# Fillers that spread the moving tiles of a fused attention and MLP kernel over eight byte remainders modulo 256

## The chip, the cores and the metric

The kernel runs on one core of a Trainium2 chip. The metric is the device time of one execution in microseconds: the median of three runs, 985.93 us, with 985.16 and 987.45 as the lowest and the highest. One more execution was profiled; every duration below comes from that one.

## The reference

Block-causal attention (4 batches, 8 heads, 576 tokens, head size 64), then a gated MLP with a sigmoid (512 to 1536 to 512), then an MLP with a leaky ReLU (512 to 2048 to 512), all in float32:

```python
scores = scale * np.matmul(q, k.transpose(0, 1, 3, 2))
scores = np.where(block_i >= block_j, scores, -1000000000.0)   # blocks of 64 positions
attn = np.exp(scores - np.max(scores, axis=-1, keepdims=True))
attn = attn / (np.sum(attn, axis=-1, keepdims=True) + 1e-09)
x = np.matmul(attn, v)            # then laid out as 2304 tokens x 512
x = (1.0 / (1.0 + np.exp(-(x @ w_gate))) * (x @ w_val)) @ w_out
h = x @ w_in
out = np.maximum(0.01 * h, h) @ w_out2
```

## The kernel before

The 2304 tokens lie along the columns of every tile, the features along the 128 partitions. They are worked on in three stages, of 768, 512 and 1024 tokens (the third as two halves of 512 that are combined by Strassen's scheme). The attention of a later batch is woven into the matmuls of the stage before it.

Every float32 number of the MLPs is split into a high and a low part of type `float32r`, side by side in one tile, and each product is three matmuls: high by high, high by low, low by high. The function `half_unit` issues twelve of them for one output tile of stages one and two (four slices of the inner dimension, line 1301); `pair_unit` issues six for one Strassen product of the third stage (line 1149). In each of these matmuls a 128x128 piece of the weight tile `w` is the stationary operand, loaded anew for every matmul, and 512 columns (256, 320 or 192 at some places of stage one) of another tile are the moving operand. Attention (`attention`, lines 428, 569, 584, 633, 657, 730, 753, 773) uses plain float32; in its transposes `ident` is moving and `both` is stationary.

A planner (`Plan.order`) sets the order of all instructions from costs and due times in the code. It knows nothing of addresses.

The tiles are allocated one pool after the other, each starting where the last one ended, in multiples of 32 bytes of a partition. `pool` and `ring` make the pools; `const` is the pool of the constants (`ident`, `mask`, `x1`, `warm`). Two fillers are there already: `warm`, of which one column is used, has 64 columns, and a pool `even` of 192 bytes stands ahead of `r_x`. With them every weight tile and every moving tile of the MLPs starts at a multiple of 256 bytes of its partition. All slices that the MLP matmuls read start at multiples of 256 bytes within their tile, and so do the slices of `w`.

Of the kernel before, what the change touches and what calls it, by code (L numbers as in the profile page):

```python
# [8 lines left out]
F32 = mybir.dt.float32  # L9
# [9 lines left out]
P = 128  # L19
# [205 lines left out]
def block_attention_then_two_mlps(  # L225
# [30 lines left out]
    def pool(name, bufs, **k):  # L256
        return ctx.enter_context(tc.tile_pool(name=name, bufs=bufs, **k))

    def ring(name, bufs, shape, dtype=F32, **k):
        return Ring(pool("p_" + name, bufs, **k), bufs, shape, dtype, name)  # L260

    out_hbm = out
    const = pool("const", 1)
    dram = pool("dram", 1, space=bass.MemoryType.DRAM)
    r_raw = ring("raw", 3, [P, 8 * P], U32)
    r_mag = ring("mag", 2, [P, 4 * P])
    r_rnd = ring("rnd", 2, [P, 4 * P], I32)
    r_wf = ring("wf", 3, [P, 4 * P])
    r_w = ring("w", 7, [P, 2, 4 * P], F32R)
    r_g = ring("g", 4, [P, 2 * SL], F32R)  # L270
    r_gf = ring("gf", 3, [P, SL])
    r_qk = ring("qk", 3, [P, 2, S])
    r_v = ring("v", 2, [P, 2, NKT, D])
# [9 lines left out]

    ident = const.tile([P, P], F32, name="ident")
    mask = const.tile([P, 4 * P + BLK], BF16, name="mask")
    x1 = const.tile([P, 4, 2, TN], F32R, name="x1")
    warm = const.tile([P, 64], F32, name="warm")
    pool("even", 1).tile([P, 48], F32, name="even")
    r_x = ring("x0", 4, [P, 2 * TN])
    r_xa = ring("xa", 2, [P, 4 * CUT])  # L290
    x0, xa, xt = [r_x.tile(F32R) for _ in range(4)], [r_xa.tile(F32R) for _ in range(2)], []
    r_sg = ring("sg", 1, [P, NSG[0] * SL])
    sg = [r_sg.tile()]

    N_PT = (NKT - 1) * 2 * 4 * P
    r_both = ring("both", 1, [P, 16 * TN])
    both = r_both.tile()
    p_t = Lazy(lambda: both[:, :N_PT].rearrange("p (j a q) -> p j a q", j=NKT - 1, a=2))

    pp, at_col = {}, N_PT  # L300
    for c, n, turns_of in ((0, P, 2), (1, 2 * P, 2), (2, 3 * P, 1), (3, 4 * P, 1), (NKT - 1, S, 1)):
# [4 lines left out]
    assert at_col <= 16 * TN  # L306
    for k, x in (("first", (3, 0, 0)), ("second", (3, 1, 0))):
        pp[k] = pp[x]
    r_acc = ring("acc", 1, [P, 4 * SL])
    acc = r_acc.tile()  # L310
    wd = [dram.tile([P, 2, 4 * P], F32, name=f"wd{u}") for u in range(NU)]
# [1193 lines left out]
```

## Time and profile before

| | us |
|---|---|
| median of three runs | 985.93 |
| the profiled execution, its own time | 985.49 |
| its span, first to last instruction | 983.7 |
| TensorE matmul busy (PE) | 968.5 |
| TensorE weight load busy (PEld) | 780.4 |
| VectorE busy (DVE) | 777.4 |
| ScalarE busy (ACT) | 549.6 |
| GpSimd busy (POOL) | 163.1 |
| granted TensorE clock, mean | 1.000 |

Consecutive matmuls overlap in the pipeline, so the duration of one (389 ns for 512 columns) is longer than the distance from its start to the next one's start. The distance is what a matmul costs; it is read from the start times in the timeline, where equal instructions that follow each other are merged into one row with their count.

### The profile page before, as it was taken

Reading aid. Unit: us, or ns where it says so; the run is one execution under the profiler, and the core shown is the slowest. Engines: PE = TensorE matmul, PEld = TensorE weight load, DVE = VectorE, ACT = ScalarE, POOL = GpSimd, SP = SyncE. Lnnn points to the kernel's source line nnn. Section 1 sums busy time; section 2 is a strip of 40 time slices with the busy share of each in tenths; the row PEclk is TensorE's granted clock in tenths of the full one; section 3 lists DMA queues with packets and bytes.
Section 4 is the critical chain, followed back from the end, with each engine's and each line's share of the span. In section 5 each row is a group of like instructions: output and inputs, shape, how many; then the busy total and the mean of one; then the engine's idle time right before and its main releaser. Section 6 shows DMA issues by size and latency. Waiting matters only on the chain.

```text
span 983.7 us, 15675 instructions
## 1 busy us (share of the span) xinstructions
PE 968.5 (98%) x5468; PEld 780.4 (79%) x5468; DVE 777.4 (79%) x1658; ACT 549.6 (56%) x1103; POOL 163.1 (17%) x172
## 2 busy tenths in 40 slices
PE   7999999999999999999999999999999999999998
PEld 4688888879888888778777877778888877888886
DVE  6989989889989847778789988985538479958656
ACT  7988776576766516455655575444526134744521
POOL 2422001221102101213432232120002021100000
PEclk9999999999999999999999999999999999999999
DMA  7488886856875636989888887877565555665664
GB/s 212 139 288 268 265 288 218 265 186 227 277 266 188 214 121 232 311 278 296 302 283 282 290 262 252 294 255 249 179 204 194 189 183 160 200 212 182 198 195 147
DMA packets 92718, 227.52 MB, mean 231 GB/s; under 512 B 9952, under 2 KB 29920, under 8 KB 92640
## 3 DMA queue, kind: packets, MB, share of 16 engines
q1 hardware_dynamic: 92640, 226.53, 69.6%
q8 instruction: 43, 0.70, 0.3%
q14 instruction: 35, 0.29, 0.1%
HBM read 150.47 MB, written 76.02 MB: 230 GB/s over the span
## 4 chain that ended last, share of the span: by engine, by line
PE 94%; DVE 2%; ACT 2%; DMA 1%; issue 0%; SPq 0%; ACTq 0%; DVEq 0%
PE mm L1301 47%; PE sc L1149 18%; PE tp L1149 9%; PE mm L1149 4%; PE tp L633 3%; PE sc L428 3%; PE pa L657 2%; PE tp L428 2%; PE tp L569 1%; DMA w<-ds 1%; PE mm L657 1%; PE tp L584 1%; ACT both L500 1%; ACT both L518 1%; DVE x L1221 0%; DMA qk<-in_qk 0%
## 5 line engine op out<-in xcount | busy, mean ns | idle before, releaser
L1301 PE MATMUL mm<-x,w 128*128 128x512 f32 (+2 forms) x1008 | 234.2, 384 | 0.0
L1301 PEld LDWEIGHTS mm<-x,w 128*128 128x128 f32 x1008 | 179.9, 188 | 38.5 <-issue 5.2
L1301 PE MATMUL mm<-g,w 128*128 128x512 f32 (+1 forms) x792 | 163.7, 358 | 0.0
L1301 PEld LDWEIGHTS mm<-g,w 128*128 128x128 f32 x792 | 130.2, 189 | 23.0 <-issue 2.4
L1149 PE MATMUL sc<-both,w 128*128 128x512 f32 x480 | 128.2, 390 | 0.1
L1149 PEld LDWEIGHTS sc<-both,w 128*128 128x128 f32 x480 | 89.9, 188 | 19.9 <-ACT wf L342 0.5
L500 ACT ACTIVATE both<-both,nm 128x256 f32<-128x256 f32 (+5 forms) x148 | 84.1, 570 | 28.3 <-DVE nm L485 27.6
L901 POOL TENSOR_TENSOR wf<-mag,rnd 128x512 int32<-128x512 int32 x28 | 37.3, 1332 | 205.9 <-DVE w L355 107.2
L887 ACT ACTIVATE mag<-raw 128x512 f32<-128x512 f32 x68 | 45.6, 671 | 42.8 <-POOL wf L901 18.1
L1301 PE MATMUL mm<-xa,w 128*128 128x256 f32 x480 | 63.6, 285 | 0.0
L1301 PEld LDWEIGHTS mm<-xa,w 128*128 128x128 f32 x480 | 60.8, 191 | 3.3 <-issue 0.8
L355 DVE TENSOR_TENSOR g<-gf,g 128x512 fp32r<-128x512 f32 (+2 forms) x73 | 56.8, 779 | 3.0 <-ACT g L342 3.0
L520 POOL TENSOR_SCALAR both<-both,r 128x256 f32<-128x256 f32 (+6 forms) x54 | 34.9, 653 | 114.3 <-DVE r L513 95.7
L342 ACT ACTIVATE g<-gf 128x512 fp32r<-128x512 f32 (+2 forms) x61 | 40.0, 657 | 24.1 <-DVE gf L1332 12.7
L518 ACT ACTIVATE both<-both,r 128x384 f32<-128x384 f32 (+6 forms) x94 | 48.7, 567 | 7.1 <-DVE r L513 7.0
L485 DVE CUSTOM_DVE_ANT_0 both<-sc,mask 128x256 f32<-128x256 f32 (+6 forms) x101 | 39.4, 423 | 16.1 <-PE sc L428 16.1
L1362 DVE TENSOR_TENSOR acc<-mm,acc 128x512 f32<-128x512 f32 (+1 forms) x60 | 35.8, 598 | 18.8 <-PE mm L1301 18.6
L1221 DVE TENSOR_TENSOR x<-sc,x 128x512 f32<-128x512 f32 x44 | 30.1, 689 | 22.3 <-PE sc L1149 22.2
L895 DVE SCALAR_TENSOR_TENSOR mag<-raw,mag 128x512 int32<-128x512 int32 x68 | 47.4, 698 | 0.3
L1301 PE MATMUL mm<-sg,w 128*128 128x512 f32 (+1 forms) x216 | 47.2, 354 | 0.0
L428 PE MATMUL sc<-qk 64*128 64x384 f32 (+5 forms) x228 | 41.9, 415 | 5.1 <-DMA qk<-in_qk 5.1
L355 DVE TENSOR_TENSOR w<-wf,w 128x512 fp32r<-128x512 f32 x68 | 46.5, 684 | 0.2
(255 smaller groups left out, 1843.7 us busy)
## 6 DMA issues: line engine op xcount, KB each, us to landing
w<-wd SPq DMA_DIRECT2D x102, 512.0 KB, 4.6
raw<-in_w SPq DMA_DIRECT2D x68, 512.0 KB, 4.4
wd<-w SPq DMA_DIRECT2D x68, 512.0 KB, 4.1
ds<-raw SPq DMA_DIRECT2D x68, 512.0 KB, 5.2
w<-ds SPq DMA_DIRECT2D x68, 512.0 KB, 4.3
qk<-in_qk SPq DMA_DIRECT2D x32, 288.0 KB, 5.7
w<-wd SPq DMA_DIRECT2D x68, 128.0 KB, 3.8
v<-in_v SPq DMA_DIRECT2D x32, 160.0 KB, 3.5
```

Source lines behind the costliest of these rows:

```text
L342: nc.scalar.activation(dst(), src(), AF.Copy)
L355: engines[e].tensor_tensor(dst(), a(), f32(b()), ALU.subtract)
L428: nc.tensor.matmul(ps[row:row + nq, col:col + nk], lhsT=tqk[half, 0, q0:q0 + nq], rhs=tqk[half, 1, k0:k0 + nk], start=True, stop=True,)
L485: nc.vector.tensor_tensor_reduce(out=pt[:, n:n + width], in0=ps[:, col:col + width], in1=mask[:, 4 * P + BLK - width:] if masked else mask ...
L500: nc.scalar.activation(pt[:, :n], pt[:, :n], AF.Exp, bias=nm[:, k - 1:k], scale=-1.0, accum_out=sm[:, i:i + 1],)
L518: nc.scalar.activation(pt[:, :n], pt[:, :n], AF.Copy, scale=r[:, i:i + 1])
L887: op("act", c_act(n), lambda: nc.scalar.activation(mag[:], words(1).bitcast(F32), AF.Abs), [raw], [mag], [raw, mag], d - 8)
L895: op("dve", c_dve(n), lambda: nc.vector.scalar_tensor_tensor(out=mag[:].bitcast(I32), in0=words(1).bitcast(I32), scalar=-0x40000000, in1=m ...
L901: engines[e].tensor_tensor(wf[:].bitcast(I32), mag[:].bitcast(I32), rnd[:], ALU.add)
L1149: nc.tensor.matmul(p[:, :n], lhsT=wt[:, wl, at * P:(at + 1) * P], rhs=view[:, xl], start=first and k == 0 and wl + xl == 0, stop=k == 1 an ...
L1301: nc.tensor.matmul(ps[:, :n], lhsT=ws[:, wl, k * P:(k + 1) * P], rhs=srcs[k]()[:, xl, hs], start=k == 0 and wl + xl == 0, stop=k == 3 and ...
L1362: op("dve", c_dve(n), lambda: nc.vector.tensor_tensor(a(), ps[:, :n], a(), ALU.add), [ps], toks_a, [ps, *host], e)
```

## The change

No instruction is added, removed or moved, and no tile changes its place in the order of allocation except `x1` and `warm`, which swap. A helper `gap(n)` opens a pool with one tile of n bytes per partition that nothing uses. `warm` shrinks to 32 columns. The fillers shift the tiles as in this table (byte addresses follow from the sizes of the tiles in order; "moving" counts the matmuls of the two MLPs that read the tile as moving operand):

| tile | start modulo 256 before | after | moving, 512 columns | moving, fewer columns |
|---|---|---|---|---|
| `w` (stationary) | 0 | 0 | - | - |
| `x1` | 0 | 128 | 720 | - |
| `g` | 0 | 192 | 762 | 264 of 256 |
| `x0` | 0 | 160 | 432 | 48 of 320, 48 of 192 |
| `xa` | 0 | 32 | 120 | 480 of 256 |
| `sg` | 0 | 64 | 186 | 72 of 256 |
| `both` | 0 | 96 | 480 | - |
| `acc` | 0 | 224 | 102 | - |
| `qk`, `raw` | 0 | 0 | 210 | - |

`x0` and `x1` both appear as `x` in the rows of the profile. In attention the moving tiles `qk`, `last` and `ident` and the stationary tile `v` keep their remainders (0, 128, 128, 0); `both` goes to 96 there too.

```diff
+    def gap(n):
+        pool(f"gap{len(gaps)}", 1).tile([P, n // 4], F32, name=f"gap{len(gaps)}")
+        gaps.append(n)
+
+    gaps = []
...
     r_w = ring("w", 7, [P, 2, 4 * P], F32R)
+    gap(192)
     r_g = ring("g", 4, [P, 2 * SL], F32R)
+    gap(64)
     r_gf = ring("gf", 3, [P, SL])
...
     mask = const.tile([P, 4 * P + BLK], BF16, name="mask")
+    warm = const.tile([P, 32], F32, name="warm")
     x1 = const.tile([P, 4, 2, TN], F32R, name="x1")
-    warm = const.tile([P, 64], F32, name="warm")
-    pool("even", 1).tile([P, 48], F32, name="even")
+    const.tile([P, 32], F32, name="gap")
+    gap(352)
     r_x = ring("x0", 4, [P, 2 * TN])
+    gap(128)
     r_xa = ring("xa", 2, [P, 4 * CUT])
...
+    gap(32)
     r_sg = ring("sg", 1, [P, NSG[0] * SL])
...
+    gap(32)
     r_both = ring("both", 1, [P, 16 * TN])
...
+    gap(128)
     r_acc = ring("acc", 1, [P, 4 * SL])
```

## Rows read from the trace of the kernel before

**Rows 1.** The page: span, busy time of the engines, granted clock in 40 slices.
```profile
span 983.7 us, 15675 instructions
PE 968.5 (98%) x5468; PEld 780.4 (79%) x5468; DVE 777.4 (79%) x1658; ACT 549.6 (56%) x1103; POOL 163.1 (17%) x172
...
PEclk9999999999999999999999999999999999999999
```

**Rows 2.** The chain that ended last, and the longest waits of PE: total us, times, longest.
```profile
PE 94%; DVE 2%; ACT 2%; DMA 1%; issue 0%; SPq 0%; ACTq 0%; DVEq 0%
...
PE sc L428 <- DMA qk<-in_qk: 5.1, 2, 4.8
PE tp L1149 <- DMA w<-ds: 2.1, 2, 1.6
PE tp L1149 <- DVE x L355: 0.9, 1, 0.9
```

**Rows 3.** Groups of matmuls by shape: xcount | busy us, mean ns of one.
```profile
L1301 PE MATMUL mm<-x,w 128*128 128x512 f32 x912 | 220.8, 394 | 0.0
...
L1149 PE MATMUL sc<-both,w 128*128 128x512 f32 x480 | 128.2, 390 | 0.1
L1301 PE MATMUL mm<-xa,w 128*128 128x256 f32 x480 | 63.6, 285 | 0.0
```

**Rows 4.** Timeline of PE, third stage: start us, us, instruction, xcount.
```profile
838.00 0.84 PE L1149 MATMUL mm<-x,w 128*128 128x512 f32 x3
838.68 2.88 PE L1149 MATMUL sc<-both,w 128*128 128x512 f32 x12
841.40 0.84 PE L1149 MATMUL tp<-xa,w 128*128 128x512 f32 x3
842.08 0.84 PE L1149 MATMUL mm<-x,w 128*128 128x512 f32 x3
...
852.28 0.84 PE L1149 MATMUL sc<-g,w 128*128 128x512 f32 x3
852.96 0.84 PE L1149 MATMUL tp<-qk,w 128*128 128x512 f32 x3
853.64 0.84 PE L1149 MATMUL sc<-both,w 128*128 128x512 f32 x3
...
859.76 0.84 PE L1149 MATMUL tp<-raw,w 128*128 128x512 f32 x3
860.44 0.84 PE L1149 MATMUL sc<-both,w 128*128 128x512 f32 x3
```

**Rows 5.** Timeline of PE, first stage, units of 256 and 512 columns in turn.
```profile
162.99 2.91 PE L1301 MATMUL mm<-x,w 128*128 128x512 f32 x12
165.74 1.59 PE L1301 MATMUL mm<-xa,w 128*128 128x256 f32 x12
167.17 2.91 PE L1301 MATMUL mm<-x,w 128*128 128x512 f32 x12
```

**Rows 6.** Duration ns min/median/max of one matmul, line 1301, from 100 to 143 us.
```profile
L1301 PE MATMUL mm<-x,w x72: 389/389/398, 100.0 to 123.5; 128*128 128x512 f32 x72
L1301 PE MATMUL mm<-xa,w x68: 277/283/386, 99.8 to 142.9; 128*128 128x256 f32 x68
```

**Rows 7.** Weight loads of the third stage, 835 to 975 us, by shape.
```profile
L1149 PEld LDWEIGHTS sc<-both,w 128*128 128x128 f32 x174 | 32.7, 188 | 6.8
```

**Rows 8.** Timeline of PE: attention scores of 288 columns, first at 0, then at 128.
```profile
32.26 0.70 PE L428 MATMUL sc<-qk 64*64 64x288 f32 x4
32.80 0.65 PE L428 MATMUL pa<-qk 64*64 64x288 f32 x4
```

**Rows 9.** Timeline, end of the program: last sum and the stores of the output.
```profile
978.32 2.79 SPq L337 DMA_DIRECT2D out_t<-x  x2
...
980.05 0.69 DVE L1221 TENSOR_TENSOR x<-sc,x 128x512 f32<-128x512 f32 x1 [1.76 <-PE sc L1149]
```

## The prediction, made before the changed kernel ran

> **What bounds the kernel now.** I read the page's busy times first, then the chain that ended last, then the waits of PE, and last the timeline of PE, because only it shows what one matmul costs. PE is busy for 968.5 of 983.7 us and its clock was granted in full, the 2.4 GHz level, in every slice [rows 1]. The chain is PE for 94%, and the longest wait that PE has on anything is 5.1 us for the first load; the next are 2.1 and 0.9 us [rows 2]. So the time is the number of matmuls times the distance from one to the next, and whatever the other engines gain or lose is hidden unless it reaches PE. The change touches exactly one thing that could alter that distance: where the moving operand starts in its partition.
>
> In the third stage 3 matmuls take 0.68 us from the first's start to the next row's first, and 12 take 2.72 us (838.68 to 841.40): 226.7 ns each [rows 4]. 512 columns at 2.4 GHz are 213.3 ns, so each matmul pays 13.3 ns more, as much as 32 columns. With units of 256 columns, 12 take 1.43 us (165.74 to 167.17), 119.2 ns each, against 106.7 for the columns [rows 5]: nearly the same extra. There are 3012 fp32r matmuls of 512 columns, so the extra holds about 40 us of the 985. This is the pot. The question is whether any of it depends on the remainder.
>
> **The change part by part.** The profiled execution took 985.49 us: a span of 983.7 and 1.8 around it. It lies 0.44 us below the median of 985.93, and the sum is made against it.
>
> *Order and fillers.* The instructions stand in the same order on every engine in both programs, so no wait is added and no queue is passed. The fillers cost no instruction. Cost 0, with no cover needed.
>
> *The matmuls whose moving tile is shifted.* By the table of the change these are 2802 of 512 columns (720 + 762 + 432 + 120 + 186 + 480 + 102), 816 of 256 and 96 of 320 or 192. The 210 that read `qk` and `raw` stay. No row of before has an fp32r matmul at a remainder other than 0, so the price per matmul is bounded from both sides.
> - Gain at most: all of the extra goes. 2802 x 13.3 = 37.3 us, 912 x 12.5 = 11.4 us, together 48.7.
> - Loss at most: the slowest undisturbed 512-column matmuls of a stretch last 398 ns, the median 389, so 9 ns more [rows 6]. 3714 x 9 = 33.4 us.
> - I take 0. The rows nearest to the question say so twice. First, `x1`, `both`, `xa`, `g`, `qk` and `raw` lie at different distances from the weights and in different places of the partition, at odd as well as even multiples of 256 bytes, and step by exactly the same 0.68 us per three [rows 4]; the extra looks like a fixed toll and not like a clash of two addresses. Second, in the plain-float32 scores of the last queries there is one pair at two remainders: the four instructions at remainder 0 take 0.70 us of busy time and the four at 128 take 0.65 [rows 8]. That pair is weak evidence: it reads slower than fp32r does (0.54 us from 32.26 to 32.80 is two passes of 288 columns side by side, 270 ns each, against 226.7 for 512), so its reads have slack to hide a clash in.
>
> What speaks against 0 is that the extra is not quite constant. After units of 256 columns, the next 12 of 512 take 2.75 us (162.99 to 165.74) instead of 2.72 [rows 5], and single durations run from 389 to 398 ns at 512 columns and from 277 to a median of 283 at 256 [rows 6]. The mean at line 1301, where units of both widths and attention alternate, is 394 ns against 390 at line 1149 [rows 3]. Nothing waits there on another engine, so how a matmul's reads fall in time against the next weight load's does change its cost. A byte offset in a stream read at a constant pace is a shift in time of a few ns, so a remainder could do the same.
>
> The Trainium skill speaks against the change here: "TensorE: Matmul & The Clock Gate", section "Step-by-step: what each phase is for", says that the moving operand and the weight load have two independent read ports, so that loading the next weights takes nothing from the running matmul. By that rule the sum is 0 whatever the remainders are. The trace agrees only in part: the 389 to 398 ns of rows 6 are not what two wholly independent streams would show.
>
> *Weight loads.* They start at 0 as before and last 188 ns, one per 226.7 ns, and begin while the previous matmul runs [rows 7]. With 512 columns there is room; with 256 the distance of 119.2 ns has little, which I count with the matmuls. Cost 0.
>
> *Attention.* The moving `qk`, `last`, `ident` and the stationary `v` keep their remainders. `both` moves to 96, as the moving operand of 192 matmuls and the stationary one of 408 transposes. Bounds: 0.05 us per four instructions as in rows 8, in either direction, over 600 is 7.5 us; nearer is 0, since that pair showed no loss.
>
> *VectorE, ScalarE, GpSimd.* They read and write the shifted tiles in some hundreds of instructions. DVE has 777 us of work in 983.7 [rows 1], and PE waits for it only about 1 us at a time [rows 2]. If 1000 instructions lost 10 ns each, 10 us of work would be added to engines with 200 us and more of slack: 0 to 1 us on the path. I take 0. If that cover failed, the add-up of a product (line 1221) would be late and PE would wait for its bank.
>
> *DMA.* `w`, `raw`, `qk` and `v` are loaded to the same remainders. The stores of the output leave from `x0`, now at 160; the last ones stand behind the last sum at 980.05 us [rows 9], so a slower store would show directly: 0 to 0.3 us, and I take 0.
>
> Sum: 985.49 + 0, so the median should stay at 985.9.
>
> **The rivals.** *Some remainders read worse (slower).* The 16 columns that pass in half of the 13.3 ns are 64 bytes, so a reader that takes 64 bytes at a time would need a 33rd piece for 512 columns that start at an odd multiple of 32: `x0`, `xa`, `both`, `acc`. These are 1134 matmuls of 512 columns and 576 shorter ones. A price from the rows: of the 12 in 2.75 us [rows 5], taking seven at 226.7, the other five cost (2.75 - 1.587) / 5 = 232.6 ns, 5.9 more. 1710 x 5.9 = 10.1 us, or 995.6. If all seven new remainders pay, 3714 x 5.9 = 21.9 us, or 1007.4. For it: the unsteady distances. Against: a start that is out of step could also settle back, as the twelve of rows 5 seem to do. It beats the forecast as soon as a matmul of these four tiles costs 1.2 ns more (2 us over 1710).
>
> *The remainders pull the two streams apart (faster).* If the extra comes from the moving stream and the weight load meeting in one place of 256 bytes, shifting one against the other shrinks it. Price: the fastest 256-column matmul is 6 ns shorter than the median one [rows 6]; 3714 x 6 = 22.3 us gives 963.2, and if only some of the tiles gain, half of that, 974.3. For it: that a shorter one exists. Against: the equal steps of rows 4, and that the extra fits 32 columns at 512 columns as at 256, which a meeting of two streams at random would not.
>
> The far end of that rival has a page: "TensorE: Matmul & The Clock Gate", section "Back-to-back issue gap", states N / 2.4 + 2.5 ns, 215.8 ns for 512 columns. If the shifted matmuls fell to that, the estimate by the page is 2802 x 10.9 = 30.5 us less, 955.0; the trace's 226.7 ns at remainder 0 does not agree with the page.
>
> *The change moves the wrong operand's neighbours.* If the shifted tiles matter only to VectorE, ScalarE or the stores, the time moves by 1 us at most; that falls within the forecast's own range, 984.5 to 987.
>
> **How the numbers follow.** No change, at 985.9: 0.46. Slower by four tiles, 0.21 around 995.6, by all of them, 0.13 around 1007. Faster: 0.20, half of it between 975 and 984 and half below. A measurement of this kernel can tell about 0.2%, 2 us, from no change. The forecast's own range is 984.5 to 987. To hold 8 in 10 the range must reach past 995.6 with the uncertainty of that price, to 1003, and down to 975; left out are about a tenth below and a tenth above. Faster 0.20, same 0.46, slower 0.34.
>
> **What would show it.** In the timeline of the third stage after the change, three matmuls of `x1`, `both`, `xa`, `g`, `acc` each have a row of their own: if all still step by 0.68 us the forecast is right. If rows of `both`, `xa` and `acc` step by 0.70 and those of `g` and `sg` by 0.68, the 64-byte rival is right; if `g` and `sg` rise too, all remainders pay. Steps of 0.65 to 0.66 mean that the streams were pulled apart. `qk` and `raw` are the control: they keep remainder 0 and should keep 0.68 in every case, unless what matters is a change of remainder from one product to the next. I would be wrong about the cover if PE's waits for DVE grew beyond a few us with equal steps.

## The result: 1.2% slower

The changed kernel takes 998.63 us (median of four runs, 997.40 to 999.92) against 986.69 (985.16 to 989.29): a ratio of 1.0118, 95% interval 1.0092 to 1.0145. The forecast of no change was wrong; the time lies inside the range of 975 to 1003.

The profiled execution took 997.40 us, its span is 995.6, 11.9 us longer than before. The page shows where it went: PE alone was busy for as much longer.

```profile
span 995.6 us, 15675 instructions
PE 980.4 (98%) x5468; PEld 778.5 (78%) x5468; DVE 780.7 (78%) x1658; ACT 549.7 (55%) x1103; POOL 163.8 (16%) x172
```

Against [rows 1] PE gained 11.9 us of busy time with the same 5468 matmuls. VectorE (DVE) gained 3.3 us and the others moved by less. The waits of PE, from its waits view, hardly changed (compare [rows 2]), so no other engine is late:

```profile
PE sc L441 <- DMA qk<-in_qk: 5.1, 2, 4.7
PE tp L1162 <- DMA w<-ds: 2.3, 2, 1.7
PE tp L646 <- ACT both L355: 0.8, 1, 0.8
```

The groups by shape (xcount | busy us, mean ns of one) say which matmuls, compared with [rows 3]:

```profile
L1314 PE MATMUL mm<-x,w 128*128 128x512 f32 x912 | 225.0, 398 | 0.0
...
L1162 PE MATMUL sc<-both,w 128*128 128x512 f32 x480 | 131.2, 396 | 0.1
L1314 PE MATMUL mm<-xa,w 128*128 128x256 f32 x480 | 62.6, 282 | 0.0
```

The 512-column matmuls went from 394 to 398 ns and from 390 to 396; the 256-column ones became shorter, 285 to 282. The timeline of the third stage (start us, us, count), which answers to [rows 4], gives the distances:

```profile
846.49 0.86 PE L1162 MATMUL mm<-x,w 128*128 128x512 f32 x3
847.20 2.97 PE L1162 MATMUL sc<-both,w 128*128 128x512 f32 x12
850.01 0.86 PE L1162 MATMUL tp<-xa,w 128*128 128x512 f32 x3
850.71 0.86 PE L1162 MATMUL mm<-x,w 128*128 128x512 f32 x3
...
861.19 0.86 PE L1162 MATMUL sc<-g,w 128*128 128x512 f32 x3
861.89 0.85 PE L1162 MATMUL tp<-qk,w 128*128 128x512 f32 x3
862.58 0.86 PE L1162 MATMUL sc<-both,w 128*128 128x512 f32 x3
```

Twelve matmuls of `both` take 2.81 us (847.20 to 850.01) instead of 2.72, three of `xa`, `x1` and `g` 0.69 to 0.71 instead of 0.68. `qk` is the surprise: it kept remainder 0 and still takes 0.69. In the first stage, against [rows 5], the 512-column units got longer (2.81 us) and those of 256 shorter (1.41 instead of 1.43):

```profile
163.25 2.97 PE L1314 MATMUL mm<-x,w 128*128 128x512 f32 x12
166.06 1.57 PE L1314 MATMUL mm<-xa,w 128*128 128x256 f32 x12
167.47 2.97 PE L1314 MATMUL mm<-x,w 128*128 128x512 f32 x12
```

The steady state is gone. Between 100 and 143 us the median 512-column matmul lasted 389 ns before, and that was also the shortest [rows 6]; now the shortest is 392 and the median 397 (duration ns, min/median/max):

```profile
L1314 PE MATMUL mm<-x,w x72: 392/397/400, 100.0 to 123.7; 128*128 128x512 f32 x72
L1314 PE MATMUL mm<-xa,w x67: 277/280/384, 99.7 to 143.0; 128*128 128x256 f32 x67
```

A matmul's duration is its distance to the next one plus about 162 ns (389 for a step of 227, 396 for 233), so single steps can be read from durations as well as from start times. Summed over the trace, the distances after 3011 of the 3012 fp32r matmuls of 512 columns (the last one has no next) grew from 698.0 to 712.1 us, and those after the 816 of 256 columns fell from 99.6 to 97.5: 14.1 - 2.1 = 12.0 us, the whole difference of the spans.

### The profile page after: what moved, and what is told of

Same layout as the page of the kernel before. It is cut to its first block, busy times and chain, and to the rows that moved or that the text cites. A ratio compares the mean times of both kernels' runs of the same rounds, so it can differ in the third digit from the quotient of the medians.

```text
span 995.6 us, 15675 instructions
## 1 busy us (share of the span) xinstructions
PE 980.4 (98%) x5468; PEld 778.5 (78%) x5468; DVE 780.7 (78%) x1658; ACT 549.7 (55%) x1103; POOL 163.8 (16%) x172
## 4 chain that ended last, share of the span: by engine, by line
PE 94%; DVE 2%; ACT 2%; DMA 1%; issue 0%; SPq 0%; ACTq 0%; DVEq 0%
PE mm L1314 47%; PE sc L1162 18%; PE tp L1162 9%; PE mm L1162 4%; PE tp L646 3%; PE sc L441 3%; PE pa L670 2%; PE tp L441 2%; PE tp L582 1%; DMA w<-ds 1%; PE mm L670 1%; PE tp L597 1%; ACT both L513 1%; ACT both L531 1%; DVE x L1234 0%; DMA qk<-in_qk 0%
## 5 line engine op out<-in xcount | busy, mean ns | idle before, releaser
L1314 PE MATMUL mm<-x,w 128*128 128x512 f32 (+2 forms) x1008 | 238.4, 388 | 0.0
L1162 PE MATMUL sc<-both,w 128*128 128x512 f32 x480 | 131.2, 396 | 0.1
```

The lines of the kernel that those rows point to most:

```text
L1162: nc.tensor.matmul(p[:, :n], lhsT=wt[:, wl, at * P:(at + 1) * P], rhs=view[:, xl], start=first and k == 0 and wl + xl == 0, stop=k == 1 an ...
L1314: nc.tensor.matmul(ps[:, :n], lhsT=ws[:, wl, k * P:(k + 1) * P], rhs=srcs[k]()[:, xl, hs], start=k == 0 and wl + xl == 0, stop=k == 3 and ...
```

## The experiments

All of them start from the kernel before and move tiles by fillers alone, unless said otherwise. "Offset" is the moving tile's remainder minus the weights', modulo 256. Three theories stood at first. A: the offset counts. B: the moving tile's own remainder counts. C: it is the mix of remainders in consecutive products.

### Everything moved by 128 (theory A against B)

```diff
+    const.tile([P, 32], F32, name="gap")
     x1 = const.tile([P, 4, 2, TN], F32R, name="x1")
```

> All tiles of the MLP matmuls, the weights too, are moved by 128 bytes, so that moving and stationary operand have the same remainder again, but not 0. Theory A, what counts is the moving operand's remainder relative to the weights': the steps in the third stage return to 0.68 us per three and the time to that of the kernel before, 985 to 988 us. Theory B, what counts is that the moving operand itself starts at a multiple of 256: steps as x1 had them after the change (232 ns against 226.7), 3012 x 5.5 ns = 16 us more, about 1000 us. Theory C, what counts is that consecutive products read different remainders: there is only one here, so 986 us.

Measured: 986.94 us, ratio 1.0001 (0.9991 to 1.0010). The third stage's timeline steps as before:

```profile
840.13 2.88 PE L1156 MATMUL sc<-both,w 128*128 128x512 f32 x12
842.85 0.84 PE L1156 MATMUL tp<-xa,w 128*128 128x512 f32 x3
843.53 0.84 PE L1156 MATMUL mm<-x,w 128*128 128x512 f32 x3
```

2.72 us for twelve and 0.68 for three. B falls: no remainder is bad in itself.

### Only the weights moved by 128 (A against B and C)

```diff
+    gap(128)
     r_w = ring("w", 7, [P, 2, 4 * P], F32R)
+    gap(128)
     r_g = ring("g", 4, [P, 2 * SL], F32R)
```

> Only the weight tiles are moved, to 128; every moving tile stays at 0. Theory A: the offset between the two is 128 for every product, 232 ns a step, 3012 x 5.5 = 16.6 us more, less 2 or 3 us on 256-column units: 998 to 1001 us. Theory B (moving operand's own remainder): no change, 986 us. Theory C: 986 us.

Measured: 1000.38 us, ratio 1.0128 (1.0113 to 1.0143). No moving tile had been touched and there is no mix, yet the timeline shows twelve matmuls of `both` in 2.80 us and three of `xa` or `x1` in 0.70:

```profile
850.05 2.96 PE L1157 MATMUL sc<-both,w 128*128 128x512 f32 x12
852.85 0.86 PE L1157 MATMUL tp<-xa,w 128*128 128x512 f32 x3
853.55 0.86 PE L1157 MATMUL mm<-x,w 128*128 128x512 f32 x3
854.25 0.86 PE L1157 MATMUL tp<-xa,w 128*128 128x512 f32 x3
```

A holds; C is not needed to lose 13 us.

### One offset for all: 64, 32 and 224

All moving tiles at 64 (fillers of 64 ahead of `x1`, 192 ahead of `r_w`, 64 ahead of `r_g`):

> All moving tiles at remainder 64, the weights at 0: one remainder for all, so no mix. Theories A and B: 512-column steps as sg had them after the change, about 230 ns, 3012 x 3.3 ns = 10 us more, less 816 x 1.5 ns = 1 us on the 256-column units; about 994 us. Theory C, the mix: 986 us as before.

Measured: 988.90 us, ratio 1.0018 (1.0009 to 1.0028). The loss is about a fifth of what was expected from `sg` in the mixed kernel. Its timeline:

```profile
840.64 2.91 PE L1158 MATMUL sc<-both,w 128*128 128x512 f32 x12
843.38 0.85 PE L1158 MATMUL tp<-xa,w 128*128 128x512 f32 x3
844.07 0.85 PE L1158 MATMUL mm<-x,w 128*128 128x512 f32 x3
```

Twelve in 2.74 us. The single steps, from the start times, run through a cycle of 225 or 226, 229, and 231 or 232 ns, with a mean of 229. So offsets are not equally bad, and the mix costs something beside: `sg` at the same offset took about 230 in the changed kernel.

Weights at 224 (offset 32; fillers of 224 ahead of `r_w` and 32 ahead of `r_g`), and weights at 32 (offset 224; 32 and 224):

> Weights at 224, all moving tiles at 0: one offset of 32 everywhere. Theory A with a smooth dependence on the distance to 0: better than 64 (988.9 us), so 986 to 988.5. Theory A with a loss as in the mixed kernel (xa at 32: 232 ns): 3012 x 5.5 = 16 us, 1000 us. The 64-byte theory of the prediction (odd multiples of 32 cost an extra piece): about 1000 us as well, but then 128 should have cost nothing, and it cost 13 us.

> Weights at 32, all moving tiles at 0: an offset of 224, the mirror image of 32. If the two streams meet symmetrically the step equals that of the weights at 224; if the order matters (the moving stream runs through its bytes faster than the weight load), it differs. From acc at 224 in the changed kernel: 233 ns, 3012 x 6 = 18 us, less 2 on the 256-column units, about 1002 us.

Measured, one run each: 1000.05 and 1001.08 us, 1.3% and 1.4% over the 986.88 of the kernel before on that chip. The mean steps at 512 columns are 233.3 and 233.2 ns. Offset 32 is as bad as 128 while 64 is mild, so the loss does not grow smoothly with the distance from 0. The 256-column units differ: 97.7 us in sum at offset 32, 99.1 at 224, 99.6 at 0.

### Weight buffers alternately at 0 and 128 (which weights count)

```diff
-    r_w = ring("w", 7, [P, 2, 4 * P], F32R)
+    r_w = ring("w", 7, [P, 8 * P + 32], F32R)
+    gap(128)
     r_g = ring("g", 4, [P, 2 * SL], F32R)
...
                     t.ap = t.ring.pool.tile(t.ring.shape, t.dtype, name=t.ring.name)
+                    if t.ring is r_w:
+                        t.ap = t.ap[:, :8 * P].rearrange("p (l n) -> p l n", l=2)
```

> The seven weight buffers alternate between remainder 0 and 128 (each is 128 bytes longer); all moving tiles at 0. Inside a unit of twelve all weights come from one buffer, so units at offset 0 and at offset 128 stand next to each other. Theory A1, the offset acts through the weight load that runs during a matmul (the next matmul's weights): the twelfth matmul of a steady unit at offset 0 already leaves 226.7 ns when the next unit's weights lie at 128. Theory A2, it acts between a matmul and its own weights: the twelfth still costs 226 to 227 and only the first of the next unit departs. Either way about four of seven units are at offset 0 but must settle again after each neighbour, so steps of about 229 to 230 on average: 697.9 + 3012 x 2.5 ns, about 993 us; if each unit had its own steady step, half of the loss of w at 128, about 993 us too.

Measured, one run: 996.22 us against 986.88, 3 us more than expected. The time tells nothing apart; the last matmul of a unit does. These are durations (ns, min/median/max, then first and last start) around 246.6 us, where a unit with weights at 0 ends and one with weights at 128 begins: three matmuls up to the last but one, the last two (the windows share one), the twelve of the next unit, and (timeline) the weight load that runs during the last matmul of the first unit:

```profile
L1308 PE MATMUL mm<-x,w x3: 389/389/389, 245.7 to 246.2; 128*128 128x512 f32 x3
...
L1308 PE MATMUL mm<-x,w x2: 389/392/396, 246.2 to 246.4; 128*128 128x512 f32 x2
...
L1308 PE MATMUL mm<-x,w x12: 390/394/404, 246.6 to 249.2; 128*128 128x512 f32 x12
...
246.40 0.19 PEld L1308 LDWEIGHTS mm<-x,w 128*128 128x128 f32 x1
```

The matmul that starts at 246.4 us still reads moving data and own weights at remainder 0, and takes 396 ns instead of 389. What is at 128 is the next matmul's weights, which are loaded while it runs: that load also starts at 246.40. Over the whole trace, from the start times, 607 matmuls of 512 columns had been steady (two steps of 226 or 227 before): 541 stayed at 226 or 227, 63 took 232 or 233, one took 230, and two waited for a load. By the order in which the kernel issues its matmuls, all 63 are the last to read their weight tile, like the one at 246.4 us. The trace does not name the buffer of the next tile, but that tile's own steps tell where it lies: two steps of 226 or 227 in a row mean 0 (the kernel with all weights at 128 has none), and a step of 240 or 241 means 128. Ahead of 512-column matmuls of the first kind all 48 last matmuls stayed at 226 or 227; ahead of those of the second kind 49 of 50 took 232 or 233, and one 230.

That leaves one doubt: is it the running matmul's data or the next one's that the loaded weights must match? Both lie at 0 here. The next run has the answer too.

### Only `xa` moved, to 192 (neighbours, and the 256-column units)

```diff
+    gap(192)
     r_xa = ring("xa", 2, [P, 4 * CUT])
+    gap(64)
     x0, xa, xt = [r_x.tile(F32R) for _ in range(4)], [r_xa.tile(F32R) for _ in range(2)], []
```

> Only xa is shifted, to 192; everything else at 0 as before. After the change the 256-column units ran at 115 ns at offset 192 (g) against 119 to 120 at offset 0. If that holds for a single tile: 480 x 4 = 1.9 us less on the first stage, 120 x 6 = 0.7 us more in the third: about 984.8 us. If the steady step at offset 0 is a state that a neighbour of another offset destroys, as qk and raw suggest (230 ns in the changed kernel, though they stayed at 0), the 512-column units between those of xa lose too: 432 x 4 = 1.7 us and up to 1400 x 4 = 5.6 us in the third stage, 988 to 992 us.

Measured: 986.03 us, ratio 0.9992 (0.9983 to 1.0002): not told apart from the kernel before. Both expected effects are in the trace and nearly cancel: over all, the 256-column sum fell by 0.9 us and that of 512 columns rose by 1.4. In the first stage `xa` went from 119.4 to 117.4 ns a step and `x0` from 228.9 to 227.8, a gain; in the third `xa` rose to 233.4, and its neighbour `both`, unmoved, from 226.9 to 228.2. Durations of the last matmuls of `both` ahead of an `xa` product at 760.6 us, and of the first ones of that product:

```profile
L1157 PE MATMUL sc<-both,w x8: 389/389/389, 758.8 to 760.4; 128*128 128x512 f32 x8
...
L1157 PE MATMUL tp<-xa,w x2: 394/394/394, 760.9 to 761.1; 128*128 128x512 f32 x2
```

The last `both`, running while the weights for the first `xa` matmul are loaded, keeps 389: so the next matmul's moving data does not matter, and in all 19 places of the trace where an `xa` matmul of 512 columns follows a steady one, that one steps by 226 or 227. Its own does: the `xa` matmul runs at 394. With the run before, that settles what must match: the data that a matmul streams, and the weights that are being loaded during it.

### Shorter weight loads (how the price depends on the load)

The matmul with the low part of the weights computes only 64 of its 128 output rows and stands second of three, in the kernel before and in the one with weights at 128 (the same edit is made for `half_unit`):

```diff
-                    for wl, xl in ((0, 0), (0, 1), (1, 0)):
+                    for wl, xl in ((0, 0), (1, 0), (0, 1)):
                         nc.tensor.matmul(
-                            p[:, :n], lhsT=wt[:, wl, at * P:(at + 1) * P], rhs=view[:, xl],
+                            p[:P - wl * D, :n], lhsT=wt[:, wl, at * P:(at + 1) * P - wl * D], rhs=view[:, xl],
...
```

> Leaves out half of the low-part products: the matmul with the low part of the weights loads and computes only the first 64 of 128 output rows, and stands second of three (all tiles at 0 as before). So the weight load that runs during every first matmul of three has 64 columns instead of 128. Theory A1 taken further, the 13.3 ns that a 512-column matmul pays at offset 0 are also the toll of the weight load that runs beside it: the first of three falls by about 6.7 ns (from 226.7 to 220), 1004 x 6.7 = 6.7 us less, about 980 us. If the 13.3 ns are a fixed price of a matmul, nothing changes: 986.9 us.

> The same half load (the same half of the low-part products left out), with all weights at 128. If each loaded column that meets the moving stream costs its share, the first of three loses half of its loss as well: against the run with the weights at 128 (1000.4 us) 1004 x (19/2) ns = 9.5 us less, about 991 us. If the loss does not depend on how much is loaded, about 1000 us.

Measured, one run each: 989.58 and 998.25 us, against one run of 986.78 of the kernel before. The loads did become shorter, 135 ns instead of 188, as the groups of the weight loads of the first of the two runs show (xcount | busy us, mean ns):

```profile
L1307 PEld LDWEIGHTS mm<-g,w 128*128 128x128 f32 x528 | 94.0, 188 | 26.5 <-issue 2.3 <-ACT both L506 0.8 <-DVE wf L947 0.2
...
L1307 PEld LDWEIGHTS mm<-x,w 128*64 128x64 f32 x336 | 45.3, 135 | 10.4
```

The matmul beside the shorter load takes 229.1 ns at offset 0, not 220, and 233.0 at 128, where 232.8 was the mean with full loads. So at 128 the loss is no price per loaded column. At offset 0 the run lasted 2.8 us longer instead of 6.7 less, and my extension of A is not borne out; but it is no clean test of the 13.3 ns, because with the uneven loads and the new order the steady 226.7 ns no longer appears and the steps wander between 224 and 236.

### Only the 256-column views of `xa` moved (a version to keep)

```diff
-    r_xa = ring("xa", 2, [P, 4 * CUT])
+    r_xa = ring("xa", 2, [P, 4 * CUT + 64])
...
-        a, c = (x[:].rearrange("p (k l n) -> p k l n", l=2, n=n) for x, n in ((xa[k // 2], CUT), (x0[k], TN)))
+        a, c = (x.rearrange("p (k l n) -> p k l n", l=2, n=n) for x, n in ((xa[k // 2][:, 48:48 + 4 * CUT], CUT), (x0[k][:], TN)))
```

> Only the 256-column views of xa in the first stage are shifted, to 192; the same buffers are read at 0 in the third stage. From the run with xa at 192 everywhere: 256-column units 117.4 instead of 119.4 (460 x 2 = 0.9 us less), 512-column units of x0 227.8 instead of 228.9 (0.5 us less), and no loss in the third stage: 1.4 us below the kernel before, 985.6 us. If the offset matters only in the third stage's products, no change: 987.0 us.

Measured: 984.97 us, ratio 0.9984 (0.9974 to 0.9993): a gain of 0.2%, whose interval ends just short of no change. Timeline of its first stage:

```profile
165.65 1.58 PE L1307 MATMUL mm<-xa,w 128*128 128x256 f32 x12
167.06 2.88 PE L1307 MATMUL mm<-x,w 128*128 128x512 f32 x12
169.78 1.46 PE L1307 MATMUL mm<-xa,w 128*128 128x256 f32 x11
```

1.41 us for twelve of 256 columns and 2.72 for twelve of 512, against 1.43 and 2.75 in [rows 5]: the offset helps the short units. Of the 25 times in the trace that a unit of 512 columns follows one of `xa`, 18 step by 226 or 227 from the first matmul on and take 2.72 us; before, none of the 25 did.

The sums of all distances, from the start times (us; they hold the few us of waits too):

| kernel | offset | 3011 of 512 columns | 816 of 256 columns |
|---|---|---|---|
| before | 0 | 698.0 | 99.6 |
| changed | eight mixed | 712.1 | 97.5 |
| everything at 128 | 0 | 697.8 | 99.6 |
| moving at 64 | 64 | 702.2 | 97.6 |
| weights at 224 | 32 | 713.3 | 97.7 |
| weights at 128 | 128 | 712.4 | 98.9 |
| weights at 32 | 224 | 713.3 | 99.1 |
| weights at 0 and 128 | 0, 128 | 707.6 | 99.6 |
| `xa` at 192 | 0, 192 | 699.4 | 98.7 |
| `xa` at 192 for 256 columns only | 0, 192 | 697.7 | 98.6 |
| shorter loads | 0 | 703.7 | 97.5 |
| shorter loads, weights at 128 | 128 | 712.2 | 97.9 |

## Why the prediction was wrong, step by step

- *What bounds the kernel*: right. The steps of PE made the whole difference.
- *Order, fillers, other engines, DMA, attention*: right at 0 as far as the time goes. The waits stand as before, VectorE's 3.3 us more stayed hidden, and the end of the program after the last sum did not change.
- *The shifted matmuls, "I take 0"*: this step failed. It rested on the equal steps of `x1`, `both`, `xa`, `g`, `qk` and `raw` [rows 4], which I read as a sign that two addresses cannot clash. But all of them stood at the same offset to the weights modulo 256, the only one that the kernel had; the rows could not show what another does. They did show that multiples of 256 are alike. What the runs showed in place of 0 is 14.1 us more on the 512-column matmuls and 2.1 us less on those of 256 columns, set by the offset between the streamed data and the weights that are loaded meanwhile. The plain-float32 pair [rows 8] showed nothing either, as the prediction feared.
- The evidence against 0 was named and under-weighed: a step that depends on how a matmul falls in time against the weight load [rows 5, 6] also told that the steps have more than one pace. That it is the same effect, seen through time instead of through addresses, is likely but not shown; what speaks for it is that moving `xa` alone brought the 2.75 us of [rows 5] down to 2.72.
- *The slower rival* had the mechanism of the cause in its heading only. Its 64-byte reader is refuted: `x1`, `g` and `sg` are no odd multiples of 32 and pay, and a uniform 64 pays least while a uniform 128 pays in full. That its 995.6 us lies near the measured time is chance. Its other branch, all remainders pay, named the right matmuls; its price of 5.9 ns stands against a measured 14.1 us / 3011 = 4.7 ns. Its sum of 21.9 us was too high mostly because it charged the shorter matmuls too (912 x 5.9 = 5.4 us), of which those of 256 columns gained 2.6 ns each.
- *The faster rival* was right for exactly those 256-column units, and wrong for the 512-column ones that are most of the time.
- *The control*: `qk` and `raw` were said to stay at 0.68 unless a change of remainder matters. They rose to about 230 ns. The run with only `xa` moved shows why: a matmul at another offset leaves its neighbours out of the steady step, and they need several matmuls to come back to it.
- The rule of the Trainium skill that I weighed, in "TensorE: Matmul & The Clock Gate", section "Step-by-step: what each phase is for", that loading the next weights takes nothing from the running matmul, does not agree with these fp32r matmuls: they take 226 or 227 ns with the next weights at 0, and 232 or 233 with them at 128.

## What to carry to other kernels

Where fp32r matmuls of 512 columns run back to back with a weight load each, as here, give moving and stationary tiles the same byte remainder modulo 256; 0 and 128 did equally well. No other kernel was tried. A filler of some bytes is worth 1.2% of the time here, and any new small tile ahead of the weights or the activations can lose it again without a trace in the order of instructions. When a profile shows that all tiles behave alike, ask whether they differ in the one thing that the change varies.

## What the runs showed of the hardware

The distance between two such matmuls depends on the offset modulo 256 between the streamed data and the weights loaded meanwhile: 226.7 ns as a steady step at 0; at one uniform offset means of 229 at 64, 233.3 at 32, 232.8 at 128, 233.2 at 224. Units of 256 columns are the other way round: those of `xa` take 119.4 at 0 and 116.7 at 64. The 226.7 ns are a state that a run of matmuls falls into: in the kernel before, after a unit of 256 columns the steps go through 233, 236, 228, 233, 231 and only then stay at 226 or 227, the same series within 1 ns in all 48 places; after attention the series is another. Why the steady step has 13.3 ns more than its columns, and why 64 is mild and 32 is not, stays open; that the loss at 128 is not proportional to the loaded columns is all that the runs say of it. Offsets that are no multiple of 32 were not tried.
